# Two stacked gated layers behind an attention stage on one core: weight pieces loaded into their final buffers, the order of work found by a planner that repeats itself, and the first token block's steps split around the second's

## The chip, the cores and the metric

The kernel runs on one core of one Trainium2 chip. The metric is the device time of that core in microseconds. Engine names are those of the profile: PE is TensorE's matmul side (PEld its weight loads), DVE is VectorE, ACT is ScalarE, POOL is GpSimd, and SP is SyncE, which here only issues DMAs.

## What is computed

Four batches of eight heads (576 positions, 64 wide) go through two attentions whose outputs are added. One is a softmax attention on q, k, v averaged over groups of four positions, its output repeated four times. The other is a local softmax attention in which a position sees only neighbours less than four away. The sum is laid out as 2304 tokens by 512. Two feed-forward layers follow (512 to 2048 and back), the first with a sigmoid gate, the second with a rational function. Cut to what matters:

```
out_up = np.repeat(sm_attn(q_d, k_d, v_d), 4, axis=2)     # on means over 4 positions
scores = np.where(abs(i - j) < 4, scale * q @ k.T, -1e9)
x = (out_up + softmax(scores) @ v).transpose(0, 2, 1, 3).reshape(2304, 512)
h = x @ moe_w_in;  x = (h * sigmoid(h)) @ moe_w_out
h = x @ moe2_w_in; out = rational(h; a, b) @ moe2_w_out
```

The large weights arrive as 64-bit floats.

## The kernel before

**Stages.** The first stage is all of the attention and the first layer, woven together; the second stage is the second layer. A matmul in it keeps single precision by three products: every operand is split into a rounded high part and a low rest, and high times high, high times low and low times high are added in PSUM.

**Steps of the first stage.** The 2304 tokens are cut into five blocks, of 480 tokens four times and 384 once (`BLOCKS1`, in chunks of 96). A **step** is one block and one of the 16 slices `f` of 128 hidden columns; there are 80 of them (`STEP1`), block by block. Step s has an h part (`h_mm`, L739, 12 matmuls into `hps`), then on ACT a tanh (L890), on DVE the product with it (L893, `th<-th,hps`, which I use as the **mark** of the step because every step has exactly one), on ACT the high part `gh` and on DVE or POOL the low part `gl` (L902). Two steps later comes the o part (`o_mm`, L751, 12 matmuls that add into `acc`). After slice 15 the block's sums are copied out of PSUM (`o_out`) and stored (`o_store`) for the second stage.

**Pieces.** Each slice of each weight matrix is one piece: 32 of the first layer (`I` for w_in, `O` for w_out) and 32 of the second. `piece` loads the raw 64-bit words into a ring `raw` of three buffers and turns them into two single-precision parts: ACT takes the high words (L651) and the low words (L655), DVE clamps and shifts (L658, L660), DVE or POOL adds (L664), DVE merges (L667), ACT makes the rounded part (L286), DVE or POOL the rest (L675). A w_in piece stays on the chip in its home `w{f}`. A w_out piece goes to a ring `wo` of three, is used by its step in block 0 and is also stored to memory (`wos`), from where the later blocks reload it, once a step. Second-layer pieces go through a single buffer `cvo` to memory.

**Attention.** Six chunks of 96 tokens a batch. A chunk has scores on PE (L522, L531), a maximum on DVE (L537), exponentials on ACT (L547), sums on DVE (L552), a normalisation on DVE or POOL (L556), transposes on PE (L567), a copy, the product with v on PE (L582), the addition of the averaged attention's output on DVE (`ad`, L589, two instructions), then the high part `xh` on ACT and the low part `xl` (L603) on DVE or POOL. A batch also has the averaged attention (L423, L439, L444, L448, L457, L471) once. A block can begin when the chunks in its 480 tokens are through.

**What sets the order.** All of this is written as jobs with costs per engine, prerequisites, buffers and a due time. `Plan.run` walks through time and gives every free engine the ready job with the earliest due time; the instructions are then emitted in that order, and each engine runs its own in program order. Due times are constants here: step s is due at `HEAD` plus the sum of the steps before it, a block's attention `LEAD` = 45000 ns ahead of the block, a piece some 6000 ns ahead of its step in block 0. While the plan sees PE empty early on, filler matmuls (`warm`, L250) are put in.

## Time and profile before

| | |
|---|---|
| time, median of 3 runs | 934.55 us (934.46 to 936.43) |
| the profiled execution's own time | 939.73 us |
| its span, first to last instruction | 937.9 us |
| busy: PE, PEld, DVE, ACT, POOL | 909.9, 762.6, 706.6, 603.0, 333.6 us |
| busy tenths of DVE in 40 slices | 6899989863457667667332289998999899799995 |
| busy tenths of PE in 40 slices | 8997888999999999999999999999999999999997 |

The profiled execution took 5.2 us more than the median, and 1.8 us of its time lies outside the span. One slice of the 40 is 23.4 us. A 9 is 90% or more. The second stage begins at about 532 us, where the mark of step 79 is. PE's ends are modelled, so a stretch in which PE shows busy may still hold short waits.

### The profile page before, as it was taken

The numbers are of one execution on the slowest core, as the hardware profiler recorded it, in microseconds if no ns is written. First come the engines' busy times: TensorE is split into PE (matmuls) and PEld (weight loads), VectorE is DVE, ScalarE is ACT, GpSimd is POOL, SyncE is SP. The second block draws the span as 40 slices with busy tenths as digits, with TensorE's granted clock in tenths as the row PEclk, the third lists the DMA queues.
The fourth block names the chain that finished last, engine by engine and source line by source line (L and its number), as shares of the span: only waits on it lengthen the run. The fifth ranks groups of instructions, "written<-read, shape, count | busy, mean of one in ns | idle before, by whom it ended". The sixth has DMA issues, their size and how long they took to land.

```text
span 937.9 us, 16163 instructions
## 1 busy us (share of the span) xinstructions
PE 909.9 (97%) x6201; PEld 762.6 (81%) x6201; DVE 706.6 (75%) x1064; ACT 603.0 (64%) x1214; POOL 333.6 (36%) x279
## 2 busy tenths in 40 slices
PE   8997888999999999999999999999999999999997
PEld 6785666787888778887899988888888888899986
DVE  6899989863457667667332289998999899799995
ACT  4877757644345666555332378877877777788884
POOL 4532232212201132213000046655555546455553
PEclk9999988999999999999999999999999999999999
DMA  9886799688978668774966573002000200200000
GB/s 281 276 232 215 222 294 292 224 316 255 246 247 286 212 227 264 236 289 148 341 216 224 181 287 151 1 1 90 0 1 9 71 1 1 78 1 1 35 1 34
DMA packets 47497, 152.03 MB, mean 162 GB/s; under 512 B 5212, under 2 KB 9948, under 8 KB 47420
## 3 DMA queue, kind: packets, MB, share of 16 engines
q1 hardware_dynamic: 44972, 143.03, 43.8%
q0 software_dynamic: 2160, 7.96, 4.9%
q8 instruction: 49, 0.80, 0.4%
q14 instruction: 28, 0.23, 0.1%
q10 hardware_dynamic: 288, 0.00, 0.0%
HBM read 116.38 MB, written 34.60 MB: 161 GB/s over the span
## 4 chain that ended last, share of the span: by engine, by line
PE 83%; DVE 6%; DMA 5%; ACT 4%; issue 1%; POOL 0%; ACTq 0%; SPq 0%; DVEq 0%; POOLq 0%
PE hps L739 39%; PE acc L965 21%; PE acc L751 17%; DMA raw<-moe_w_in 3%; DMA raw<-moe_w_out 2%; DVE cw L667 1%; ACT E L547 1%; PE wps L250 1%; PE pair L531 1%; PE pair L582 1%; DVE cr L664 1%; ACT EE L439 1%; DVE cw L660 1%; DVE cw L658 1%; PE pair L567 1%
## 5 line engine op out<-in xcount | busy, mean ns | idle before, releaser
L751 PE MATMUL acc<-gh,wo 128*128 128x480 f32 (+1 forms) x640 | 204.8, 378 | 7.0 <-ACT wo L286 3.7
L739 PE MATMUL hps<-xh,w 128*128 128x480 f32 (+1 forms) x640 | 208.1, 384 | 1.0 <-ACT w L286 0.4
L739 PE MATMUL hps<-x2h,wi 128*128 128x512 f32 (+1 forms) x640 | 196.4, 368 | 0.0
L819 POOL TENSOR_TENSOR u<-u,ah 128x512 f32<-128x512 f32 (+1 forms) x80 | 96.1, 1201 | 261.7 <-ACT u L817 260.0
L965 PE MATMUL acc<-wo,gh 128*128 128x512 f32 x576 | 178.0, 390 | 0.0
L751 PEld LDWEIGHTS acc<-gh,wo 128*128 128x128 f32 x640 | 119.0, 188 | 27.5 <-ACT wo L286 5.7
L739 PEld LDWEIGHTS hps<-xh,w 128*128 128x128 f32 x640 | 121.1, 191 | 20.6 <-DVE w L675 1.3
L739 PEld LDWEIGHTS hps<-x2h,wi 128*128 128x128 f32 x640 | 118.9, 188 | 16.4
L996 POOL TENSOR_TENSOR gl<-p,gh 128x512 fp32r<-128x512 f32 (+1 forms) x80 | 120.9, 1511 | 11.6 <-issue 8.8
L965 PEld LDWEIGHTS acc<-wo,gh 128*128 128x128 f32 x576 | 107.7, 188 | 20.9
L739 PE MATMUL hps<-xl,w 128*128 128x480 f32 (+1 forms) x320 | 120.4, 376 | 0.0
L751 PE MATMUL acc<-gl,wo 128*128 128x480 f32 (+1 forms) x320 | 118.5, 370 | 0.0
L739 PE MATMUL hps<-x2l,wi 128*128 128x512 f32 (+1 forms) x320 | 117.7, 368 | 0.0
L965 PE MATMUL acc<-wo,gl 128*128 128x512 f32 x288 | 112.7, 391 | 0.0
L893 DVE SCALAR_TENSOR_TENSOR th<-th,hps 128x480 f32<-128x480 f32 (+1 forms) x80 | 50.4, 629 | 68.4 <-ACT th L890 67.8
L988 DVE SCALAR_TENSOR_TENSOR u<-u,r 128x512 f32<-128x512 f32 (+1 forms) x80 | 99.4, 1243 | 2.8
L890 ACT ACTIVATE th<-hps 128x480 f32<-128x480 f32 (+1 forms) x80 | 44.5, 557 | 87.5 <-PE hps L739 84.8
L981 ACT ACTIVATE r<-u,cst 128x512 f32<-128x512 f32 (+1 forms) x80 | 54.5, 682 | 52.7 <-POOL u L819 52.7
L987 DVE SCALAR_TENSOR_TENSOR u<-u,r 128x512 f32<-128x512 f32 (+1 forms) x80 | 83.5, 1043 | 0.5 <-ACT r L982 0.5
L664 POOL TENSOR_TENSOR cr<-cw,cr 128x512 int32<-128x512 int32 x25 | 33.8, 1353 | 137.4 <-DVE cw L660 96.6
L816 DVE TENSOR_TENSOR p<-p,hps 128x512 f32<-128x512 f32 (+1 forms) x80 | 50.5, 632 | 30.4 <-ACT p L815 30.3
L286 ACT ACTIVATE gh<-th 128x480 fp32r<-128x480 f32 (+1 forms) x79 | 46.6, 590 | 38.6 <-DVE th L893 27.4
(122 smaller groups left out, 1468.8 us busy)
## 6 DMA issues: line engine op xcount, KB each, us to landing
wo<-wos SPq DMA_DIRECT2D x64, 512.0 KB, 4.2
raw<-moe_w_in SPq DMA_DIRECT2D x32, 512.0 KB, 4.7
raw<-moe_w_out SPq DMA_DIRECT2D x32, 512.0 KB, 5.9
w2s<-cvo SPq DMA_DIRECT2D x32, 512.0 KB, 5.6
kq<-kq SPq DMA_DIRECT2D x12, 788.0 KB, 7.8
wos<-wo SPq DMA_DIRECT2D x16, 512.0 KB, 4.7
wi<-w2s SPq DMA_DIRECT2D x16, 512.0 KB, 7.8
wo<-w2s SPq DMA_DIRECT2D x16, 512.0 KB, 7.4
```

The costliest lines, as they stand in the source:

```text
L286: nc.scalar.activation(out, in_, AF.Copy, scale=scale)
L739: nc.tensor.matmul(hps[:, :n], lhsT=wi[:, i, 128 * g:128 * g + 128], rhs=(a, b)[s][:, g, :n], start=(m == 0), stop=(m == len(mms) - 1))
L751: nc.tensor.matmul(acc_t[j][g // 2][:, g % 2, :n], lhsT=wo[:, i, 128 * g:128 * g + 128], rhs=s_[:, :n], start=(f == 0 and m % 3 == 0), sto ...
L816: nc.vector.tensor_tensor(out=p, in0=p, in1=hps, op=ALU.mult)
L819: nc.gpsimd.tensor_tensor(out=u, in0=u, in1=ah, op=ALU.mult)
L890: nc.scalar.activation(x["t"][:, :n], x["h"][:, :n], AF.Tanh, scale=0.5)
L893: nc.vector.scalar_tensor_tensor(out=x["t"][:, :n], in0=x["t"][:, :n], scalar=1.0, in1=x["h"][:, :n], op0=ALU.add, op1=ALU.mult)
L965: nc.tensor.matmul(acc2[j][c], lhsT=a[:, 128 * c:128 * c + 128], rhs=wo[:, i, :], start=(f == 0 and m % 3 == 0), stop=(f == NF - 1 and m % ...
L981: nc.scalar.activation(r, u, AF.Ln, scale=2.0 ** -64, bias=cst[:, 0:1])
L987: nc.vector.scalar_tensor_tensor(out=u, in0=u, scalar=1.000001, in1=r, op0=ALU.add, op1=ALU.mult)
L988: nc.vector.scalar_tensor_tensor(out=u, in0=u, scalar=-2.0, in1=r, op0=ALU.add, op1=ALU.mult)
L996: nc.gpsimd.tensor_tensor(out=gl2[k_][:, :n], in0=p, in1=gh2[k_][:, :n], op=ALU.subtract)
```

## The change

- **Homes.** A raw piece is loaded straight into the buffer in which its result will lie: `w{f}` for a w_in piece, one of `NBUF` = 7 general buffers (`buf`) for any other. These 7 take the place of `raw` (3), `cvo` (1) and `wo` (3), at the same size in total; evicted block sums use them too. The conversion overwrites the raw words in place.
- **Plan.** Due times are now relative to the planned start of a step (`At`). Only the last job of a chain has one; `run` passes it back along the prerequisites, so that each job is due as late as its successors allow. `settle` plans six times, each time with the step starts that the last plan gave, and takes the plan whose PE work ends first. A reload of a `wo` piece is tied to the o part four steps before it (`AHEAD`).
- **Split.** Block 0 runs slices 0 to 7, then block 1 all 16, then block 0 slices 8 to 15, then blocks 2 to 4. Slices 8 to 15 are thus first used in block 1. Block 0's sums are copied out twice; the second time POOL issues DMAs that add to memory.
- **Addition on PE.** In batch 0 PE adds the averaged attention's output into the same PSUM tile by two matmuls with an identity (L634 of the new kernel) ahead of the product with v. `ad` is gone there, `xh` and `xl` are taken from PSUM, `xl` always on DVE.

```
+SPLIT = 8
+AHEAD = 4
...
-RING = 3
+NBUF = 7
...
-LEAD = 45000.0
+TAIL, STAG, STAG0 = 40000.0, 4000.0, 2000.0
+TAIL1 = 24000.0
+SAFE = 4000.0
+PRE = 3000.0
...
+UP_PE = 1
+ROUNDS = 6
...
+    def settle(self, when, rounds):
+        best, tried = None, []
+        for _ in range(rounds):
+            self.run(when)
+            tried.append((max(j.end for j in self.jobs if j.eng == "P"), len(tried), when))
+            when = [j.start for j in self.jobs if j.step is not None]
+        return self.run(min(tried)[2])
...
+        for j in reversed(self.jobs):
+            for d in j.after:
+                d.t = min(d.t, j.t - self.LAT - min(d.cost.values()) -
+                          (d.size / self.DMA_RATE + self.DMA_LAT + PRE if d.size else 0.0))
...
-            pool.sort(key=lambda j: j.due)
+            pool.sort(key=lambda j: j.t)
...
+    PART1 = [(0, 0, SPLIT), (1, 0, NF), (0, SPLIT, NF)] + [(j, 0, NF) for j in range(2, len(BLOCKS1))]
+    STEP1 = [(j, f) for j, lo, hi in PART1 for f in range(lo, hi)]
+    part1 = [p for p, (j, lo, hi) in enumerate(PART1) for f in range(lo, hi)]
+    first1 = [STEP1.index((0 if f < SPLIT else 1, f)) for f in range(NF)]
...
-        due0 = when[first * NF] - LEAD
+        d0 = FAR
...
-            d0 = when[j * NF] - LEAD + 250.0 * i
+            due = begin[j] - (TAIL1 if j == 1 else TAIL) - (STAG if j else STAG0) * (BLOCKS1[j] - 1 - i)
...
+                if b < UP_PE:
+                    for a in range(2):
+                        nc.tensor.matmul(op[:, a, :2 * CH], lhsT=ident,
+                                         rhs=upt[0].rearrange("p (m a) q -> p a m q", a=2)[:, a, :, 24 * c:24 * c + 24]
+                                         .unsqueeze(3).to_broadcast([128, 2, 24, 4]), start=True, stop=False)
...
-                                                 start=True, stop=True)
+                                                 start=b >= UP_PE, stop=b >= UP_PE or m + s_ == 2)
...
+                if b < UP_PE:
+                    x["x"] = x["o"][:, :, :2 * CH].rearrange("p a (m q) -> p a m q", m=2)
+                    sl = slice(CH * i, CH * i + CH)
+                    x["h"], x["l"] = (t[j].rearrange("p (m a) q -> p a m q", a=2)[:, :, :, sl] for t in (xh, xl))
+                else:
+                    x["h"], x["l"] = (t[j][:, :, CH * i:CH * i + CH] for t in (xh, xl))
+                copy(e, x["h"], x["x"])
+            def lo(e, x=x):
+                eng(e).tensor_tensor(out=x["l"], in0=x["x"], in1=x["h"], op=ALU.subtract)
...
+            ja = jo if pe else plan.add(f"A{b}{c}", d0, {"V": 2 * v_ns(192)}, ad, after=[jo], give=[pO, upu])
+            jh = plan.add(f"H{b}{c}", d0, {"A": a_ns(384), "V": v_ns(384)} if pe else {"A": a_ns(384, False), "V": 300}, hi, port=not pe, after=[ja] + x_first.get(j, []),
...
-    for name, n in (("raw", 3), ("cw", 3), ("cr", 2), ("cvo", 1), ("wo", RING)):
+    for name, n in (("buf", NBUF), ("cw", 3), ("cr", 2)):
...
+    def buf(u, name, shape=(128, 2, DM), dtype=F32R):
+        return cv.tile(list(shape), dtype, tag=f"buf{u.no}", name=name, bufs=1)
...
-            x["raw"] = cv.tile([128, DM, 2], I32, tag="raw", name="raw", bufs=3)
+            if home.ring == "buf":
+                x["raw"] = buf(home, "raw", (128, DM, 2), I32)
+            else:
+                x["raw"] = wp.tile([128, DM, 2], I32, tag=home.ring, name="raw")
...
-        j0 = plan.add(f"{name}.l", due - 12000, {"D": 60}, ld, take=[ru] + ([dst_unit] if dst_unit in wo_u.values() else []),
-                      size=128 * 4096)
...
+        j0 = plan.add(f"{name}.l", FAR, {"D": 60}, ld, take=[home], size=128 * 4096)
...
+        j7 = plan.add(f"{name}.7", due - SAFE, {"V": 610, "G": 1270}, c7, after=[j6], give=[wu], port=True)
...
+        p = part1[s]
+        f0, f1 = PART1[p][1:]
...
+                             start=(f == f0 and m % 3 == 0), stop=(f == f1 - 1 and m % 3 == 2))
...
+    def o_store(p, i):
+        j, f0, _ = PART1[p]
         n = BLOCKS1[j] * CH
-        if g % 2 == 0:
-            xe_t[j, g // 2] = cv.tile([128, 2, DM], F32, tag="raw", name="xe", bufs=3)
-        copy(e, xe_t[j, g // 2][:, g % 2, :n], acc_t[j][g // 2][:, g % 2, :n], 0.5)
-    def o_store(j, i):
-        n = BLOCKS1[j] * CH
-        nc.sync.dma_start(out=x2s[2 * i:2 * i + 2, :, tok0[j]:tok0[j] + n].rearrange("g p n -> p g n"),
-                          in_=xe_t[j, i][:, :, :n])
+        o = x2s[2 * i:2 * i + 2, :, tok0[j]:tok0[j] + n].rearrange("g p n -> p g n")
+        if f0:
+            nc.gpsimd.dma_start(out=o, in_=xe_t[p, i][:, :, :n], accum_op=ALU.add)
+        else:
+            nc.sync.dma_start(out=o, in_=xe_t[p, i][:, :, :n])
...
+                        stores[j, g // 2] = plan.add(f"x{p}.s{g}", due, {"G": 1000} if f0 else {"D": 60},
+                                                     lambda e, p=p, i=g // 2: o_store(p, i),
+                                                     after=cps[-1:] + ([stores[j, g // 2]] if f0 else []), give=[xu],
+                                                     size=128 * 4096, early=1e9)
...
-                                       after=[wos_job[f], wo_job[NF - 1]], take=[wo_u[s]], size=128 * 4096)
+                                       after=[wos_job[f]], take=[wo_u[s]], size=128 * 4096)
...
+        for s in range(AHEAD, ns):
+            f = STEP1[s][1]
+            j = load_wo[f] if s == first1[f] else wos_load[s]
+            if s - AHEAD in done_o:
+                j.after.append(done_o[s - AHEAD])
...
-    order = plan.run()
+    order = plan.settle(guess, ROUNDS)
```

Three places show how instructions moved. The first is DVE from the mark of step 10 on. In the kernel before (`cw`, `cr`, `raw`, `w`, `wo` are pieces, `xs`, `n`, `r`, `E` attention):

```order
L893 SCALAR_TENSOR_TENSOR th<-th,hps 128x480
L658 TENSOR_SCALAR cw<-cw 128x512
L660 TENSOR_SCALAR cw<-cw 128x512
L675 TENSOR_TENSOR w_1907<-cw,w_1907 128x512
L902 TENSOR_TENSOR gl<-th,gh 128x480
L664 ISA cr<-cw,cr 128x1024
L537 TENSOR_REDUCE n_1936<-pair 128x8
L667 SCALAR_TENSOR_TENSOR cw<-raw,cr 128x512
L282 CAST wo<-cw 128x512
L675 TENSOR_TENSOR wo<-cw,wo 128x512
L552 TENSOR_REDUCE r_1980<-E_101 128x8
L553 RECIPROCAL r_1980<-r_1980 128x8
```

And the same place in the changed kernel, where step 10 is block 1's slice 2 (L986 is the mark, L995 `gl`, L739 to L756 pieces):

```order
L986 SCALAR_TENSOR_TENSOR th<-th,hps 128x480
L995 TENSOR_TENSOR gl<-th,gh 128x480
L756 TENSOR_TENSOR w_1881<-cw,w_1881 128x512
L748 SCALAR_TENSOR_TENSOR cw<-raw,cr 128x512
L739 TENSOR_SCALAR cw<-cw 128x512
L741 TENSOR_SCALAR cw<-cw 128x512
L986 SCALAR_TENSOR_TENSOR th<-th,hps 128x480
L756 TENSOR_TENSOR w_1919<-cw,w_1919 128x512
L745 ISA cr<-cw,cr 128x1024
L995 TENSOR_TENSOR gl<-th,gh 128x480
```

Before, these rows do not yet reach the mark of step 11; after, they pass it.

The second place is SP around the first reloads of w_out pieces (`wo<-wos`). Before:

```order
L643 DMA raw<-moe_w_out 128x1024
L714 DMA wos<-wo 128x1024
L643 DMA raw<-moe_w_in 128x1024
L643 DMA raw<-moe_w_out 128x1024
L723 DMA w2s<-cvo 128x1024
L865 DMA wo<-wos 128x1024
L714 DMA wos<-wo 128x1024
L865 DMA wo<-wos 128x1024
```

After:

```order
L724 DMA raw<-moe_w_in 128x1024 x2
L795 DMA wos<-wo 128x1024
L568 DMA vw<-vw 128x512 x2
L958 DMA wo<-wos 128x1024
L724 DMA raw<-moe_w_in 128x1024
L795 DMA wos<-wo 128x1024
L958 DMA wo<-wos 128x1024
L443 DMA vd<-vp 72x1024
L958 DMA wo<-wos 128x1024
```

The first reload moved from the 84th DMA on SP to the 49th, with 20 of the first layer's 32 raw pieces issued ahead of it instead of all 32.

The third place is PE at batch 0's first product with v, before the first step. Before, with filler around it:

```order
L250 LDWEIGHTS wz
L250 MATMUL wps<-wz 128x256
L582 MATMUL pair<-PT,vw_288 64x48 x16
L582 MATMUL acc<-PT,vw_288 64x48 x16
L250 LDWEIGHTS wz
```

After:

```order
L634 MATMUL pair<-up,ident 128x192 x2
L643 MATMUL pair<-PT,vw_288 64x48 x16
L634 MATMUL acc<-up,ident 128x192 x2
L643 MATMUL acc<-PT,vw_288 64x48 x16
L634 MATMUL pair<-up,ident 128x192 x2
```

Two identity matmuls now precede each product, and the first five chunks' products stand in one run.

## Rows read from the trace of the kernel before

**Rows 1.** Busy time by stretch: us, each engine's busy (instructions), PEclk, DMA share, GB/s.

```profile
50.30:107.00 56.70, 48.53 (x346) 36.08 (x344) 53.31 (x96) 39.87 (x91) 16.92 (x16) 1.00 0.69 215
107.00:179.00 72.00, 63.49 (x621) 48.42 (x620) 62.85 (x114) 48.98 (x114) 24.86 (x21) 0.91 0.87 267
179.00:224.90 45.90, 45.90 (x295) 37.73 (x294) 24.21 (x44) 21.75 (x41) 3.51 (x3) 1.00 0.88 290
224.90:317.30 92.40, 92.40 (x619) 76.88 (x617) 55.39 (x99) 46.34 (x100) 16.60 (x15) 1.00 0.80 255
317.30:468.00 150.70, 149.19 (x1287) 121.41 (x1284) 95.65 (x179) 83.23 (x201) 33.35 (x27) 1.00 0.72 247
468.00:532.20 64.20, 64.20 (x363) 63.58 (x362) 19.11 (x34) 17.34 (x35) 0.00 (x0) 1.00 0.66 228
...
0.00:201.00 201.00, 179.27 (x1893) 138.99 (x1894) 173.31 (x323) 136.37 (x345) 67.69 (x76) 0.97 0.82 258
```

**Rows 2.** First of these stretches, L893 (the marks) alone: DVE busy (count).

```profile
50.30:107.00 56.70, 5.17 (x8) 1.00 0.69 215
```

**Rows 3.** Waits of PE, 50.3 to 179 us: who, for whom, us, times, longest.

```profile
PE acc L751 <- ACT wo L286: 3.7, 5, 1.3
PE pair L567 <- DVE xs L589: 3.4, 2, 2.6
PE acc L751 <- DVE wo L675: 1.8, 4, 0.8
```

**Rows 4.** DVE's groups by line and shape: xcount | busy us, mean ns | idle before.

```profile
L667 DVE SCALAR_TENSOR_TENSOR cw<-raw,cr 128x512 int32<-128x512 int32 x64 | 47.3, 740 | 2.5 <-POOL cr L664 2.2
L893 DVE SCALAR_TENSOR_TENSOR th<-th,hps 128x480 f32<-128x480 f32 x64 | 41.5, 648 | 29.3 <-ACT th L890 28.7
L902 DVE TENSOR_TENSOR gl<-th,gh 128x480 fp32r<-128x480 f32 x54 | 37.8, 700 | 23.4 <-ACT gh L286 23.1
...
L660 DVE TENSOR_SCALAR cw<-cw 128x512 int32<-128x512 int32 x64 | 28.9, 452 | 2.2
...
L664 DVE CUSTOM_DVE_ANT_0 cr<-cw,cr 128x1024 uint16<-128x1024 uint16 x39 | 27.4, 704 | 0.5
...
L552 DVE TENSOR_REDUCE r<-E 128x8 f32<-128x440 f32 x24 | 14.6, 607 | 8.0 <-ACT E L547 7.9
...
L589 DVE TENSOR_TENSOR xs<-pair,up 128x192 f32<-128x192 f32 x42 | 13.0, 351 | 11.6 <-PE pair L582 11.4
...
L603 DVE TENSOR_TENSOR xl<-xs,xh 128x384 fp32r<-128x384 f32 x20 | 12.1, 606 | 2.6 <-ACT xh L286 2.4
...
L675 DVE TENSOR_TENSOR wo<-cw,wo 128x512 fp32r<-128x512 f32 x12 | 8.5, 712 | 0.1
...
L444 DVE TENSOR_REDUCE r<-EE 128x6 f32<-128x870 f32 x8 | 8.4, 1048 | 0.8 <-ACT EE L439 0.8
```

**Rows 5.** Timeline of PE: attention's groups of matmuls (start us, us).

```profile
30.55 1.20 PE L471 MATMUL pair<-PT,vd 72*64 72x144 f32 x16 [0.21 <-ACT PT L286]
...
41.35 0.69 PE L531 MATMUL pair<-kq 64*64 64x54 f32 x32
...
42.95 0.68 PE L582 MATMUL acc<-PT,vw 54*64 54x48 f32 x32
...
78.19 0.97 PE L423 MATMUL pair<-kqd 64*64 64x144 f32 x24
...
100.20 0.45 PE L457 MATMUL pair<-ident,EE 48*72 48x48 f32 x12 [0.29 <-ACT EE L439]
```

**Rows 6.** Chain of work that ended last: start us, us, what.

```profile
260.16 2.60 PE acc L751 x12
```

**Rows 7.** Timeline of PE where the granted clock fell.

```profile
136.34 0.66 PE L567 MATMUL pair<-ident,E 48*128 48x48 f32 x8 [2.60 <-DVE xs L589]
...
140.48 1.17 PE L739 MATMUL hps<-xh,w 128*128 128x480 f32 x2
```

**Rows 8.** Busy time by stretch there, columns as in rows 1.

```profile
130.00:140.00 10.00, 6.74 (x100) 4.86 (x91) 6.89 (x16) 5.12 (x11) 4.54 (x4) 0.77 0.93 297
```

More of the change, by code (lines that the diff above doesn't have):

```diff
@@ L84, in __init__, with run @@
     def __init__(self):
-        self.jobs, self.rings, self.lent = [], {}, {}
+        self.jobs, self.sizes, self.lends = [], {}, {}
     def ring(self, name, n):
-        self.rings[name] = list(range(n))
+        self.sizes[name] = n
     def add(self, *a, **k):
         j = Job(*a, **k)
-        for u in j.give:
-            u.left += 1
         self.jobs.append(j)
         return j
-    def run(self):
+    def settle(self, when, rounds):
[5 more added lines that the diff above has]
+        return self.run(min(tried)[2])
+    def run(self, when):
         users = {}
+        self.rings = {k: list(range(n)) for k, n in self.sizes.items()}
+        self.lent = dict(self.lends)
         for j in self.jobs:
+            for u in j.give:
+                u.left = 0
+        for j in self.jobs:
+            j.start = j.end = j.eng = None
+            j.t = when[j.due.step] + j.due.ns
+            for u in j.give:
+                u.left += 1
+        for j in reversed(self.jobs):
+            for d in j.after:
+                d.t = min(d.t, j.t - self.LAT - min(d.cost.values()) -
+                          (d.size / self.DMA_RATE + self.DMA_LAT + PRE if d.size else 0.0))
             j.wait = len(j.after)
@@ L347, in ld @@
                 nc.sync.dma_start(out=kqt[t], in_=kq[b, t])
-            loads.append(plan.add(f"L{b}{t}", due0 - (9000 if b == 0 else 0) + 100 * t, {"D": 60}, ld, take=[u],
+            loads.append(plan.add(f"L{b}{t}", FAR, {"D": 60}, ld, take=[u],
                                   size=128 * 4 * 1576))
@@ L363, in sm @@
                         nc.vector.tensor_reduce(out=o, in_=i.rearrange("p g (j r) -> p g j r", r=4), axis=AX.X, op=ALU.add)
-                    sums.append(plan.add(f"R{b}{t}{w}", due0 - 6000, {"V": v_ns(768)}, sm, after=[loads[t]] + sums[:1],
+                    sums.append(plan.add(f"R{b}{t}{w}", FAR, {"V": v_ns(768)}, sm, after=[loads[t]] + sums[:1],
                                          take=[] if sums else [kdu], give=[kqu[t]]))
@@ L624, in attention @@
             x_done.setdefault(j, []).append(
-                plan.add(f"X{b}{c}", d0, {"V": v_ns(384), "G": g_ns(384)}, lo, after=[jh], give=[xu], port=True))
+                plan.add(f"X{b}{c}", due, {"V": v_ns(384)} if pe else {"V": v_ns(384), "G": g_ns(384)}, lo, after=[jh],
+                         give=[pO] if pe else [xu], port=not pe))
+    takes = {}
     xh, xl, x_u, x_first, x_done = {}, {}, {}, {}, {}
@@ L670, in c6 @@
         def c6(e):
-            x["hl"] = dst()
+            x["hl"] = dst(home)
             copy(e, x["hl"][:, 0], x["w"])
@@ L744, in o_mm @@
         n = BLOCKS1[j] * CH
-        if f == 0 and lo == 0:
-            acc_t[j] = [ps.tile([128, 2, 512], F32, tag="acc", name="acc", bufs=2) for _ in range(2)]
+        p = part1[s]
+        f0, f1 = PART1[p][1:]
+        if f == f0 and lo == 0:
+            acc_t[p] = [ps.tile([128, 2, 512], F32, tag="acc", name="acc", bufs=2) for _ in range(2)]
         wo, gh, gl = wo_t[s], gh_t[s], gl_t[s]
@@ L832, in o_jobs @@
             n = BLOCKS1[j] * CH
-            due = when[s] + 2.2 * (when[1] - when[0])
-            if f == 0:
-                accs[j] = [Unit("acc"), Unit("acc")]
+            due = when[s] + 12000
+            p = part1[s]
+            f0, f1 = PART1[p][1:]
+            if f == f0:
+                accs[p] = [Unit("acc"), Unit("acc")]
             for i in range(4):
@@ L912, in moe1 @@
                 prev_h = plan.add(f"h{s}.{i}", when[s] + i, {"P": r_ns(n, 3)}, hm, after=after, take=[hu] if i == 0 else [],
-                                  give=[x_u[j]] if f == NF - 1 and i == 3 else [], closes=s == 0)
+                                  give=[x_u[j]] if f == NF - 1 and i == 3 else [], closes=s == 0, step=s if i == 0 else None)
             jt = plan.add(f"th{s}", when[s], {"A": a_ns(n)}, th, after=[prev_h], take=[tu])
```

157 lines of the change are left out of this document (89 added, 68 removed).

## The prediction

> **What bounds the kernel now.** I read the page's slices first: DVE stands at 8 or 9 from the second to the eighth slice while PE dips in the fourth to the seventh, and after that PE is full. So I cut the first stage at the marks (one L893 per step) of steps 0, 8, 16, 24, 40, 64 and 79 and asked for busy time in each stretch [rows 1]. The marks alone show that the first stretch holds eight steps [rows 2]. Its 56.7 us have DVE busy 53.31 and PE 48.53; the next eight steps take 72.0 us with DVE busy 62.85. From 179 us on PE is busy all the time but for 1.51 us in the stretch 317.3 to 468.0. What PE waits for in steps 0 to 15 is mostly weight pieces (`wo`) from ACT and DVE, and once for 2.6 us the addition `xs` [rows 3]. So DVE sets the pace of block 0, where all 32 first-layer pieces must be converted within 16 steps, and PE sets it after that.
>
> **PE's own need.** Twelve matmuls of 480 columns take 2.60 us [rows 6], so a step costs 5.2 us, and a step of 384 columns 4.2. Attention's groups come on top [rows 5]: scores 0.69, product with v 0.68, averaged scores 0.97, its product with v 1.20, a group of transposes 0.45; for a chunk's band matmuls I take 0.36, my estimate from half of a score group. I counted the matmuls between marks in both kernels' order. In the three stretches from 179.0 to 468.0, where PE was the bound, these durations give 249.5 us of steps and 35.0 of attention; busy was 45.9 + 92.4 + 149.2 = 287.5, that is 38.0 for attention, so I raise attention by 9%. Before, steps 0 to 8 need 39.1 us of h and o parts and 6 of attention, 45 in all, and steps 8 to 16 need 39.1 + 16 = 55. Against 56.7 and 72.0 that is 11.6 and 17 us lost, and 1.5 later: **30 us in all**. More than these 30 the change cannot take from the first stage, and it does not touch the second.
>
> **Split, part by part.** What moves is when DVE must have done what. The changed order, priced by rows 4, has between marks 0 and 8: 28 clamps and shifts (12.7 us), 10 adds L664 (7.0), 13 merges (9.6), 7 rests (5.0), 8 marks (5.2), 7 `gl` (4.9), 8 `ad` (2.8), 5 `xl` (3.0), 8 maxima and sums of attention with their reciprocals (7.4, a maximum taken like the sum), 3 normalisations (2.7, taken like the sums of the same sizes): 60.3 us. The same count before gives 58.2 for this stretch and 65.3 for the next; busy was 53.31 and 62.85, because neighbours overlap, so such a sum is worth 0.94 of itself. The changed kernel then needs of DVE 56.7 us for steps 0 to 8, and (sums 27.3, 43.7, 73.9, 103.7) 26, 41, 70 and 98 for steps 8 to 16, 16 to 24, 24 to 40 and 40 to 64. ACT, by the same counting, sums to 55.9 in the first stretch against 47.5 before, worth 47.
>
> So the crowd does not leave steps 0 to 8: attention for block 1 has moved into them (ten chunks' outputs are through by mark 8, six before) while the number of merged pieces is 18 against 17. It leaves steps 8 to 16, which hold 6 merges and no attention.
>
> PE's need in the changed order, counted the same way: steps 0 to 8: 39.7 + 15.1 = 54.8; 8 to 16: 38.4; 16 to 24: 41.7 + 6.0 = 47.7; 24 to 40: 83.3 + 20.9 = 104.2; 40 to 64: 124.5 + 19.6 = 144.1; 64 to 79: 63.2. That is 452.4, as before (451.7): nothing is saved on PE.
>
> **The waits that stay.** In steps 0 to 8 DVE (56.7) and PE (54.8) are nearly equal. Before, the stretch took 3.4 us more than DVE's busy time when PE had slack, and the next one 9.2 more. I take 6, between the two and nearer the first, where the clock held: 62.7, with bounds of 57 and 66. In steps 8 to 16 there is one new thing, the turn from block 0 to block 1: the accumulators must be copied out before block 1's o part begins. Its bounds are 0, as at the later turns, where PE showed full [rows 1], and 2.6, the longest wait of PE [rows 3]; I take 1.5: 39.9. Steps 16 to 24 then have DVE at 41 of 47.7 and ACT as full: I add 1.0. Steps 24 to 40 hold more attention than before and the second eviction: 1.2 more. Steps 40 to 64 keep the 1.5 of before. Sum: 62.7 + 39.9 + 48.7 + 105.4 + 145.6 + 63.2 = 465.5 against 481.9: **16.4 us less**.
>
> **Edits that I cost at little.** Loading into homes removes no instruction; it frees loads from the ring of three, and what it is worth is in the stretches above. The split adds two copies on ACT and two on DVE and two adding DMAs on POOL, behind which a `gl` and a piece are queued; POOL is busy 16.60 of 92.40 us where they fall [rows 1], and the second stage reads their result some 200 us later. The identity matmuls: no row shows one. Nearest are 8 matmuls of 144 columns in 1.20 us (0.20 for 192 columns) and 12 in 0.97 (0.11); upward, four passes at the 480-column rate would be 0.35. For two of them 0.2 to 0.7 us. Five of the six chunks stand before step 0, where PE runs filler; the sixth costs at most 0.7 inside steps 0 to 8. They spare DVE the two `ad` of 0.35 a chunk, but `xl` is now always DVE's (0.61) [rows 4]. Before mark 0 the DVE sum falls from 44.8 to 42.7 and ACT's from 46.0 to 45.7, so the first step may begin up to 2 us earlier, or as much later if the product with v now waits on PE's run of identities: I take 1 earlier.
>
> Together 17.4 us. The profiled execution, 939.73, would be 922.3; that run lies 5.2 above the median, so against the median 934.55 I forecast **917** (own range 911 to 924).
>
> **Rivals.**
>
> *The first eight steps stay crowded.* Three engines close to full, each in program order, could lose as steps 8 to 16 did before: 72.0 for 55 of PE, that is 17. Then steps 0 to 8 take 72 and the gain is 8: 927. For it speaks that ACT's sum grew by 8; against it that the clock's fall is part of those 17.
> *Memory.* By the reload of step 24 the changed kernel must have moved 48 MB on SP's queue and some 7 MB of adding DMAs on POOL's (sizes and places from the order), 55 MB; by my stretches that reload is due near 201 us, 274 GB/s. Before, 258 GB/s was reached to that point with the DMA engines 82% busy, and 290 at 88% at best over a long stretch [rows 1]; at full share that is 315 to 330. If no more than the 258 of before is reached, step 24 comes 12 us late: 929. The Trainium skill (DMA: Bandwidth & Descriptors, Specifications) puts the memory limit of a core at about 358 GB/s; by that, an estimate, 55 MB take 154 us and nothing would wait. No stretch of rows 1 comes above 290, so the row is the stricter one.
>
> *It closes up better.* With 57 in the first stretch and no new waits, the sum is 455 and the time 906.
>
> *Slower: the clock.* After PE waited 2.6 us, two of its matmuls spanned 1.17 us [rows 7], where 2.60 for twelve makes 0.43 and a tail, and the granted clock averaged 0.77 over 10 us [rows 8]: the lower of its two levels, 1.2 GHz, for part of it. If waits of that length come in each of steps 2 to 8, half of the stretch's 54.8 us of PE work at the lower level costs 27 us and eats the gain: 945. It decides from about 17 us of PE work at the lower level. Against it: in 50.3 to 107 PE waited often, but shortly, and the granted clock was 1.00 [rows 1]. The Trainium skill (TensorE: Matmul & The Clock Gate, What's actually happening) has the lower clock as the default and activity as what releases it; by that rule a fuller PE, as forecast here, keeps 2.4 GHz, and rows 1 agree with it.
>
> **How the numbers follow.** Forecast 0.53; better 0.13; crowded 0.14; memory 0.11; slower 0.09. Of the crowded and memory cases about a fifth would end within 0.2% (1.9 us, about what a measurement of this kernel can tell from no change). So faster 0.86, same 0.05, slower 0.09. The range reaches to the better case's 905 and past the crowded and memory cases to 930.
>
> **What would show it.** In the changed profile, the stretch between marks 0 and 8 should take 60 to 66 us with DVE busy near 57, that from 8 to 16 about 40 with PE full and DVE near 26, and mark 24 should come near 201 us instead of 224.9. Waits of PE for `wo` and `w` after 115 us should be gone. I am wrong if mark 8 comes after 118 us (crowded), if PE waits for `wo` from a DMA between 115 and 200 us (memory), if the granted clock dips before mark 24, or if new waits turn up past step 24, where I have allowed under 3 us.

## The result and the profile after

The changed kernel takes 925.63 us (median of 4 runs, 923.69 to 929.13), the kernel before, measured beside it, 935.11 (4 runs, 934.46 to 936.43): a ratio of 0.9898, 95% interval 0.9880 to 0.9916, or 9.5 us less. The forecast was 917 with a range of 905 to 930. The profiled execution of the changed kernel took 925.38 us, its span is 923.6 us (before 937.9).

The marks (start of the product with the tanh, now L986, in us from the start of the span):

| mark of step | 0 | 8 | 16 | 24 | 40 | 64 | 79 | from there to the end |
|---|---|---|---|---|---|---|---|---|
| before | 50.3 | 107.1 | 179.0 | 224.9 | 317.3 | 468.0 | 532.2 | 405.6 |
| after | 51.5 | 114.3 | 152.3 | 202.0 | 309.4 | 453.4 | 516.6 | 407.1 |

The stretches between these marks, in the form of [rows 1]: start and end, length, busy time (instructions) of PE, PEld, DVE, ACT and POOL, the granted clock, the DMA engines' share, GB/s.

```profile
51.50:114.30 62.80, 58.69 (x580) 44.96 (x579) 56.36 (x102) 46.97 (x105) 21.38 (x19) 0.97 0.78 252
114.30:152.30 38.00, 38.00 (x176) 32.82 (x175) 25.35 (x45) 19.42 (x35) 6.76 (x7) 1.00 0.98 314
152.30:202.00 49.70, 48.45 (x356) 39.43 (x354) 43.62 (x73) 37.31 (x92) 21.65 (x15) 1.00 0.70 244
202.00:309.40 107.40, 105.59 (x960) 84.55 (x959) 72.83 (x127) 61.55 (x153) 31.53 (x27) 1.00 0.85 263
309.40:453.40 144.00, 144.00 (x1134) 118.31 (x1134) 97.75 (x175) 79.67 (x173) 20.33 (x16) 1.00 0.80 278
453.40:516.60 63.20, 63.20 (x357) 62.59 (x356) 17.95 (x33) 16.28 (x33) 0.00 (x0) 1.00 0.55 191
```

The stretch of steps 8 to 16, which took 72.0 us, takes 38.0 with PE never idle; those of steps 0 to 8, 16 to 24 and 24 to 40 have become longer, the first by 6.1 us, and the last two shorter, by 6.7 and 1.0. What PE waits for in steps 0 to 24, in the form of [rows 3]:

```profile
PE pair L472 <- ACT EE L488: 1.7, 1, 1.7
PE acc L834 <- DVE gl L995: 1.4, 1, 1.4
PE pair L520 <- ACT PT L333: 0.7, 1, 0.7
...
PE hps L820 <- DVE th L986: 1.2, 1, 1.2
```

No wait for `wo` is left. After mark 24 come two more (1.2 us with no releaser, 0.6 for `PT`), after mark 40 none. The second stage did not change: from its first h matmul (518.93 us, before 533.55) to the end it takes 404.67 us (404.35), with PE busy 399.55 in both. Of the 1.5 us more in the last column of the table, 1.1 are o parts that now stand behind mark 79 (518.93 is 2.4 us behind it, 533.55 was 1.3), about as much as steps 64 to 79 take less.

### The profile page after: what moved, and what is told of

It is laid out like the page before. It is cut to its first block, busy times and chain, and to the rows that moved or that the text cites. A ratio compares the mean times of both kernels' runs of the same rounds, so it can differ in the third digit from the quotient of the medians.

```text
span 923.6 us, 16147 instructions
## 1 busy us (share of the span) xinstructions
PE 906.0 (98%) x6189; PEld 762.9 (83%) x6189; DVE 708.9 (77%) x1047; ACT 605.7 (66%) x1222; POOL 339.7 (37%) x282
## 4 chain that ended last, share of the span: by engine, by line
PE 90%; DVE 5%; ACT 3%; issue 1%; DMA 1%; POOL 0%; SPq 0%; ACTq 0%; DVEq 0%; POOLq 0%
PE hps L820 42%; PE acc L1067 21%; PE acc L834 20%; PE pair L643 1%; PE wps L290 1%; PE pair L582 1%; PE pair L520 1%; DVE cw L748 1%; ACT E L598 1%; PE pair L618 1%; ACT EE L488 1%; DMA raw<-moe_w_in 1%; DVE gl L995 0%; PE pair L506 0%; DVE cw L741 0%
## 5 line engine op out<-in xcount | busy, mean ns | idle before, releaser
L820 PE MATMUL hps<-xh,w 128*128 128x480 f32 (+1 forms) x640 | 224.4, 380 | 1.2 <-DVE th L986 1.2
L834 PE MATMUL acc<-gh,wo 128*128 128x480 f32 (+1 forms) x640 | 223.8, 378 | 0.0
L834 PEld LDWEIGHTS acc<-gh,wo 128*128 128x128 f32 x640 | 120.3, 188 | 17.4 <-issue 1.6
L983 ACT ACTIVATE th<-hps 128x480 f32<-128x480 f32 (+1 forms) x80 | 44.6, 557 | 108.3 <-PE hps L820 105.4
L986 DVE SCALAR_TENSOR_TENSOR th<-th,hps 128x480 f32<-128x480 f32 (+1 forms) x80 | 50.3, 629 | 82.0 <-ACT th L983 81.5
L745 POOL TENSOR_TENSOR cr<-cw,cr 128x512 int32<-128x512 int32 x27 | 36.7, 1361 | 119.2 <-ACT cr L736 38.8
L820 PEld LDWEIGHTS hps<-x2l,wi 128*128 128x128 f32 x320 | 60.1, 188 | 8.8
```

The costliest lines, as they stand in the source:

```text
L745: eng(e).tensor_tensor(out=x["r"], in0=x["w"].bitcast(I32), in1=x["r"], op=ALU.add)
L820: nc.tensor.matmul(hps[:, :n], lhsT=wi[:, i, 128 * g:128 * g + 128], rhs=(a, b)[s][:, g, :n], start=(m == 0), stop=(m == len(mms) - 1))
L834: nc.tensor.matmul(acc_t[p][g // 2][:, g % 2, :n], lhsT=wo[:, i, 128 * g:128 * g + 128], rhs=s_[:, :n], start=(f == f0 and m % 3 == 0), st ...
L983: nc.scalar.activation(x["t"][:, :n], x["h"][:, :n], AF.Tanh, scale=0.5)
L986: nc.vector.scalar_tensor_tensor(out=x["t"][:, :n], in0=x["t"][:, :n], scalar=1.0, in1=x["h"][:, :n], op0=ALU.add, op1=ALU.mult)
```

## A ledger of PE's lost time

The experiments become readable with three numbers a kernel, taken up to mark 79. **Idle** is the length of a stretch less PE's busy time in it. **Clock** is the time lost to the lower granted clock: one less the granted clock, times the length, added over pieces of about 5 us. What is left of mark 79 after both is what the profile shows as PE's work, fillers included. Each row is one profiled execution; the last column is the median of the kernel's runs.

| kernel (us) | idle: head, 0-8, 8-16, 16-79 | clock: head, 0-8, 8-16, 16-79 | mark 79 | less both | time, median |
|---|---|---|---|---|---|
| before | 5.1, 8.2, 8.5, 1.5 | 0, 0, 6.8, 0 | 532.2 | 502.1 | 935.11 |
| before, again | 4.7, 6.5, 9.6, 0.4 | 1.7, 0, 6.8, 0 | 530.6 | 500.9 | 936.00 |
| **after** | 5.3, 4.1, 0, 3.0 | 1.7, 1.7, 0, 0 | 516.6 | 500.8 | 925.63 |
| copies | 5.1, 4.1, 0, 3.0 | 1.7, 1.7, 0, 0 | 516.2 | 500.6 | 925.25 |
| no identity | 7.9, 4.1, 0, 0 | 0, 1.7, 0, 0 | 514.3 | 500.6 | 925.05 |
| no split (16) | 5.2, 2.9, 8.9, 0 | 1.7, 0, 3.4, 0 | 525.1 | 503.0 | 933.68 |
| split at 6 | 6.5, 8.9, 0, 1.4 | 1.7, 6.9, 0, 0 | 524.7 | 499.3 | 934.21 |
| split at 10 | 6.1, 6.7, 4.3, 0.9 | 0, 5.1, 3.4, 0 | 527.3 | 500.8 | 937.05 |
| clamp twice | 4.6, 5.8, 0.3, 6.1 | 0, 5.1, 0, 3.4 | 525.1 | 499.8 | 934.50 |
| no clamp | 6.0, 3.5, 0, 2.6 | 1.7, 0, 0, 0 | 513.3 | 499.5 | 923.44 |
| ACT twice | 4.4, 7.2, 0, 5.1 | 5.1, 3.3, 0, 1.7 | 527.7 | 500.9 | 936.92 |
| fill one wait | 5.0, 3.4, 0, 3.0 | 1.7, 0, 0, 0 | 514.9 | 501.8 | 923.69 |
| fill two waits | 5.8, 3.4, 0, 3.0 | 0, 0, 0, 0 | 515.8 | 503.6 | 925.64 |
| fill, no identity | 7.9, 2.4, 0, 0 | 0, 3.4, 0, 0 | 516.1 | 502.4 | 923.25 |

The work is 499 to 504 us in every one of them, while mark 79 moves by 18.9 us. So most of what a variant gained or lost up to mark 79 is idle time and clock, and the clock's share comes in portions of about 1.7 us. Differences of a few us in the last but one column are not explained by this. Of the 15.6 us by which mark 79 came earlier, 10.9 are idle time, 3.4 are clock, and 1.3 are the difference in the last but one column.

## The experiments

**The kernel before once more**, for the spread of its executions.

> The kernel before once more, unchanged. Theory (its profiled execution was a bad sample): its span of 937.9 us went with a granted clock of 0.993, and the other executions lie 4 to 5 us lower; then the spans and clocks listed for the new runs fall on a line, a lower clock with a longer span, the median stays near 935 us, and a new profile shows steps 8 to 16 shorter than 71.9 us, because part of those was the clock's fall at 133 to 150 us. Rival (profiling itself costs 5 us): the new profile is again near 938 us with the same fall.

936.00 us (12 runs, 933.78 to 939.88), ratio 0.9997 (0.9982 to 1.0011); the profiled span is 936.2, and steps 8 to 16 take 72.2 us again, with 6.8 of clock in them. So the theory fell where it called that stretch a bad sample: both profiled executions have its falls. It also fell in the line of clock and span: at a granted clock of 0.995 alone, the spans of these 12 runs go from 931.9 to 938.0 us. Not every execution loses as much: a clock of 0.996, which some have, leaves some 4 us for all falls together, where the ledger has 6.8 and 8.5. The rival, a cost of profiling, is not borne out either: the profiled executions of the changed kernel, of the kernel without identity matmuls and of that without the clamp lie below their medians. What stands is that the execution that the sum was made against, 939.73, was near the top of what this kernel does: all its other runs lie between 932.33 and 940.71, and the medians of their groups between 934.6 and 936.3.

**Memory: extra copies.**

```
 nc.sync.dma_start(out=new_wo(s), in_=wos[f])              # L958, reload of step s
+if s < 24: nc.sync.dma_start(out=xtra[s], in_=wos[f])     # 8 of them, memory to memory
```

> Behind each of the 8 reloads of a weight tile for steps 8 to 15 (line 958) SP issues a copy of the same 512 KB in memory that nobody reads: 4 copies in the stretch of steps 0 to 8 and 4 in that of steps 8 to 16, each read and written. Theory (the DMA engines have room though they show a share of 0.98 in steps 8 to 16, where PE is never idle): marks 8, 16 and 24 move by less than 2 us each and the time by less than 2. Rival (314 GB/s in that stretch is all there is): 2 MB read and 2 MB written at 314 GB/s are 6 to 13 us; marks 16 and 24 come 6 to 13 us later, with PE waiting for weight tiles from a DMA.

925.25 us (4 runs, 923.29 to 925.57), 0.9875 (0.9859 to 0.9890). The stretch of steps 8 to 16 in this kernel:

```profile
114.00:151.90 37.90, 37.90 (x176) 32.75 (x175) 24.96 (x44) 19.23 (x35) 7.57 (x8) 1.00 1.03 357
```

It moved 357 GB/s where the changed kernel moved 314, and PE was still never idle. A reload landed 13.3 us after its issue (median) instead of 9.0, and nothing waited for it. The DMA share of 0.98 was no limit; the memory rival falls, and by a margin. The Trainium skill (DMA: Bandwidth & Descriptors, Specifications) gives about 358 GB/s as a core's limit. This run came up to that over 37.9 us, and the changed kernel goes above it in its head, so over 10 us it does not hold here:

```profile
20.00:25.00 5.00, 3.91 (x68) 2.82 (x67) 4.93 (x8) 4.93 (x21) 4.63 (x7) 1.00 1.00 380
25.00:30.00 5.00, 4.16 (x96) 3.03 (x92) 4.17 (x10) 4.91 (x17) 3.28 (x2) 1.00 1.01 407
```

**The identity matmuls.** `UP_PE = 0`: the averaged output is added on DVE in the first batch too.

> The changed kernel with the addition in batch 0 back on DVE (UP_PE 0); homes, plan and split stay. Theory: the identities take 0.65 to 0.85 us a chunk on PE, five of them in one run on the way to step 0, and spare DVE about 0.7 a chunk, so the two cancel: within 3 us of the changed kernel's 925.6, and mark 0 within 2 us of 51.5. Rival (the identities delay the start): mark 0 comes 3 us earlier or more and the time falls to 922 or less. Other rival (they carry part of the gain): 929 or more.

925.05 us (4 runs, 923.16 to 926.94), 0.9873 (0.9850 to 0.9896): no difference from the changed kernel that these runs can tell. Their price does show, in the chain of work of the changed kernel (start us, us, what):

```profile
36.68 0.85 PE acc L634 x4
...
52.18 0.65 PE pair L634 x4
```

0.65 to 0.85 us a chunk, five of the six on the chain that leads to the first step. In the ledger PE is idle 2.6 us longer in the head without them, but loses 1.7 less to the clock there, and 3.0 us of idle time after mark 16 are gone. That they spare the wait for `ad`, and that the two cancel, fits this but was not tested by itself.

**No split.** `SPLIT = 16`: block 0 whole, then block 1; homes and new plan as they are.

> The changed kernel with block 0 run in one piece (SPLIT 16); homes, plan and identities stay, the plan is made anew for it. Theory (the split carries the gain, because it takes half of the pieces out of block 0): steps 0 to 16 take at least 118 us instead of 101 and the time is 932 to 938. Rival (the plan and the homes carry it): 924 to 928, with steps 0 to 16 below 106 us.

933.68 us (9 runs, 931.07 to 936.07), 0.9965 (0.9949 to 0.9981). Its first two stretches:

```profile
51.40:97.40 46.00, 43.10 (x249) 34.34 (x248) 45.27 (x84) 32.23 (x63) 10.39 (x10) 1.00 0.91 281
97.40:172.80 75.40, 66.45 (x685) 50.80 (x685) 64.81 (x116) 52.69 (x136) 24.80 (x21) 0.95 0.80 256
```

121.4 us for steps 0 to 16, where the changed kernel takes 100.8 and the one before 128.7. Some of the difference is attention that then lies later (steps 16 to 24 take 42.2 us here, 49.7 with the split), but 6 to 8 of the 9.5 us hang on the split (6 by the two ratios, 8 by the medians); homes, plan and identity matmuls together are worth 2 to 5 us without it. The theory was right about both numbers. No run has the split without the homes or without the repeated plan, so what each of these adds to it is not shown.

**Other places for the split.** `SPLIT = 6` and `SPLIT = 10`.

> The first block is split after 6 steps instead of 8. Steps 0 to 5 and 12 to 21 then bring new weight pieces. Theory (what counts is how many pieces and how much of attention DVE must finish in the first stretch): DVE's 56.4 us fall by 4 pieces and two steps' marks and `gl`, some 12 us, PE's by 10, so the ratio of the two stays near that of now and the ten steps with new pieces later have DVE near 51 of 58 us: 923 to 928, no clear difference from the split at 8. Rival (an earlier block 1 is short of attention's output): PE waits for `xh`, `xl` before step 6, 928 to 934.

> The first block is split after 10 steps instead of 8. With the split at 6 PE was idle 8.9 us in the first eight steps and the clock's falls took 6.9 there. Theory (what an earlier block 1 brings forward is attention for it; a later one gives ACT and DVE two more steps of PE's time for the same groups, but two more steps of pieces): idle time of PE in steps 0 to 10 stays near the 4.1 us of now, time 923 to 928. Rival (the split at 8 is a lucky order, and any other loses some 8 us, as at 6 and at 16): 931 to 936.

934.21 us (7 runs, 932.46 to 934.67), 0.9972 (0.9961 to 0.9982) at 6, and 937.05 us (10 runs, 935.18 to 938.21), 1.0003 (0.9986 to 1.0021) at 10. My theory fell both times: it counted how much the engines have to do in a stretch, and by that count all three splits are alike. The stretches of steps 0 to 8 at 6, and of steps 0 to 8 and 8 to 16 at 10:

```profile
53.30:120.90 67.60, 58.65 (x488) 44.87 (x489) 59.17 (x102) 45.25 (x95) 17.84 (x15) 0.90 0.80 254
```

```profile
48.80:118.70 69.90, 63.25 (x619) 48.80 (x620) 59.79 (x105) 47.42 (x118) 25.18 (x20) 0.93 0.75 240
118.70:167.10 48.40, 44.07 (x277) 36.62 (x276) 33.04 (x62) 25.68 (x58) 7.53 (x7) 0.93 0.82 273
```

What PE waited for in the first stretches, at 6 and then at 10:

```profile
PE hps L820 <- DVE th L986: 3.0, 1, 3.0
PE hps L820 <- ACT xh L333: 2.0, 1, 2.0
PE hps L820 <- DVE w L756: 1.6, 1, 1.6
```

```profile
PE pair L643 <- ACT E L598: 4.1, 2, 2.9
PE pair L573 <- ACT EE L488: 3.5, 1, 3.5
PE hps L820 <- DVE th L986: 3.0, 1, 3.0
```

Single waits of 1.6 to 3.5 us, nearly each for something else, with the clock falling behind most of them. At 6 the rival's wait is among them: the 2.0 us for `xh`, at 107 us, hold the first h part of block 1, and 0.4 for `xl` follow, of 8.9 us idle. Idle and clock together take 15.8 us of steps 0 to 16 at 6 and 19.5 at 10, against 5.8 at 8. So a split is not worth this by itself; this split in the order that the planner happens to find for it is. Why that order meets fewer late producers than its neighbours was not settled.

**DVE from both sides.** The clamp of a piece (L739, DVE) issued twice, and left out.

```
 nc.vector.tensor_scalar(out=x["w"], in0=x["w"], scalar1=W_LOW, scalar2=W_HIGH, op0=ALU.max, op1=ALU.min)
+nc.vector.tensor_scalar(the same)       # clamp twice; in the other kernel the first line is gone
```

> The changed kernel with the clamp of each piece (0.44 us on DVE) done twice, order of all else kept; the second clamp changes nothing in the result. Steps 0 to 8 hold 14 of the 64, 6.2 us. Theory (DVE sets the pace of steps 0 to 8): that stretch grows by 5 to 6.5 us, steps 8 to 16 by under 1, the rest together by under 4; time 931 to 936. Rival (PE or waits between engines set it): under 3 us there, time under 929.

> The clamp of a piece (line 739, the first of two DVE instructions of that step) is left out; weights below 2^-15 are then not rounded as the reference has them. It is the mirror of the doubled clamp: 14 times 0.418 = 5.9 us less of DVE in steps 0 to 8. Theory (DVE is late there, PE next): the stretch of 62.8 us falls by 3 to 5, to 58 to 60, where PE's own 54.8 to 58.7 us stop it; steps 16 to 40, where the doubled clamp cost 6, give back at most the 1.2 and 1.8 us in which PE is idle. Whole time 918 to 922. Rival (the engines are balanced and the doubled clamp only made a new bound): nothing changes, 924 to 926.

Twice: 934.50 us (10 runs, 931.85 to 936.74), 0.9981 (0.9965 to 0.9998). Without: 923.44 us (4 runs, 922.20 to 925.28), 0.9861 (0.9844 to 0.9878). The first stretch, twice and without:

```profile
50.10:117.00 66.90, 61.06 (x576) 46.77 (x577) 63.31 (x116) 46.29 (x104) 21.89 (x19) 0.92 0.78 247
```

```profile
51.20:111.10 59.90, 56.39 (x575) 43.25 (x574) 51.55 (x89) 46.64 (x106) 21.09 (x19) 1.00 0.83 259
```

With 7 us more of DVE the stretch grows by 4.1, which is 1.7 more of idle time, 3.4 more of the clock and 1.0 less of the rest; with 4.8 us less it shrinks by 2.9, of which 1.7 are one fall of the clock less and 0.6 idle time. More work on DVE does delay PE; less work gives back little, because PE itself has 56 to 57 us of work there. The time rose by 8.9 us; mark 79 came 8.5 later, with 4.4 more of idle time, 5.1 more of the clock and 1.0 less of the rest. In steps 40 to 79 the doubled clamp costs nothing (207.4 us, after 207.1), but steps 16 to 40 take 6.1 us more, where the theory had under 4 for all the rest. Steps 16 to 24 of that kernel:

```profile
154.60:208.40 53.80, 50.05 (x358) 40.51 (x360) 48.85 (x85) 37.55 (x92) 21.25 (x15) 0.97 0.63 228
```

So the forecast time of 931 to 936 came, but with less than forecast in the first stretch. Without the clamp the stretch came as the theory had it (58 to 60), and the time lies between the theory's 918 to 922 and the rival's 924 to 926.

**ACT.** Its conversion of a piece's low words (L736) issued twice.

```
 nc.scalar.activation(x["r"], x["raw"][:, :, 0].bitcast(U32), AF.Copy, scale=2.0 ** -29)
+nc.scalar.activation(the same)
```

> ACT's conversion of a piece's low half (line 736, `cr` from `raw`) is issued twice; DVE's and PE's work is unchanged. Theory (DVE sets the pace of steps 0 to 8 and ACT has room: busy 46.97 of 62.80 us there): about 14 more conversions fall into steps 0 to 8, some 8 us of ACT, of which at most 2 us show in that stretch, and 0 to 4 us in the whole time. Rival (ACT paces these steps as much as DVE, because it stands in every piece's chain): the stretch grows by 5 to 8 us and the time by 7 to 10, as with the doubled clamp on DVE (+4.1 and +8.9).

936.92 us (10 runs, 935.08 to 937.58), 1.0002 (0.9990 to 1.0014): the whole gain is gone. The first stretch, and that of steps 16 to 24:

```profile
55.30:121.20 65.90, 58.70 (x557) 44.38 (x550) 57.16 (x102) 54.86 (x119) 21.59 (x19) 0.95 0.80 249
159.70:212.70 53.00, 50.02 (x354) 40.72 (x352) 43.80 (x73) 45.18 (x104) 20.82 (x15) 0.97 0.64 231
```

The stretch grew by 3.1 us, short of the rival's 5 to 8, but the head grew by 3.8 and steps 16 to 24 by 3.3, and the whole by 11.3. So the theory that ACT has room falls, though it was busy for only 46.97 of 62.80 us. Here the idle time of an engine that runs in program order was not a reserve, since its results are waited for one by one. Of mark 79's 11.1 us, 4.3 are idle time and 6.7 clock.

**Fillers against the falls.** In the changed kernel, 2 us at a time (columns as above):

```profile
80.00:82.00 2.00, 1.81 (x29) 1.12 (x27) 1.97 (x4) 2.00 (x4) 1.83 (x2) 1.00 0.11 45
82.00:84.00 2.00, 1.26 (x21) 0.98 (x17) 2.00 (x3) 1.39 (x4) 0.40 (x1) 1.00 0.40 158
84.00:86.00 2.00, 1.91 (x15) 1.01 (x15) 1.97 (x5) 1.52 (x4) 0.00 (x0) 0.64 1.02 307
86.00:88.00 2.00, 2.00 (x14) 1.64 (x9) 1.97 (x5) 1.13 (x2) 0.00 (x0) 0.51 0.95 364
88.00:90.00 2.00, 2.00 (x20) 1.48 (x19) 1.85 (x4) 0.97 (x2) 0.00 (x0) 1.00 1.03 414
```

PE is partly idle up to 84 us; the clock falls to 0.5, that is to 1.2 GHz, after PE is busy again, and the work that was waited for then runs at half speed. The edit puts matmuls of no use ahead of waits that were seen in the trace; one kernel fills a wait in step 5, the next also one in the head.

```
+FILL = {"S11": (13, None), "t101": (2, 5), "o10": (6, 5)}   # job: fillers, step whose hps takes them
 ...
+if x.name in FILL: warm(n, into the accumulator that this step's h part will overwrite)
 x.emit(x.eng)
```

> 8 filler matmuls (128 x 256 in bf16, 0.11 us each) are put into PE's program in step 5, 2 before a group of transposes and 6 before the product with the averaged v that waited 0.74 us for ACT at 82.08 us; they write an accumulator that the next h part overwrites. Nothing else changes. In the changed kernel PE was busy 3.07 of the 4 us from 80 to 84, and from 84.4 to about 88 the granted clock was near 0.5, which cost 1.7 us. Theory (the clock falls after a stretch in which PE was partly idle, and the fall costs as much again as the wait): no fall near 85 us, the stretch of steps 0 to 8 is 1 to 2 us shorter, time 923.5 to 925. Rival (the fall has nothing to do with this wait): the fall stays, and the fillers that do not fit the wait add 0 to 0.4 us.

923.69 us (6 runs, 923.24 to 925.15), 0.9866 (0.9840 to 0.9891). The stretch of steps 0 to 8, the same 4 us and those after:

```profile
51.00:112.60 61.60, 58.16 (x586) 44.48 (x586) 55.92 (x101) 46.99 (x105) 21.99 (x19) 1.00 0.80 258
...
80.00:82.00 2.00, 2.00 (x28) 1.36 (x23) 1.97 (x4) 2.00 (x5) 1.73 (x2) 1.00 0.04 14
82.00:84.00 2.00, 1.94 (x21) 1.18 (x18) 2.00 (x4) 1.39 (x3) 0.00 (x0) 1.00 0.68 240
84.00:86.00 2.00, 1.72 (x17) 1.19 (x18) 1.93 (x5) 1.51 (x4) 0.00 (x0) 1.00 0.99 277
86.00:88.00 2.00, 2.00 (x20) 1.47 (x19) 2.00 (x5) 1.26 (x3) 0.00 (x0) 1.00 1.01 372
```

The fall is gone, and the stretch of steps 0 to 8 takes 61.6 us instead of 62.8. The time is 1.9 us lower by the medians, but the intervals of the two ratios overlap. The place is what tells: a fall stands there, between 84 and 90 us, in all three profiles of the split at 8 without fillers and with the clamp and ACT's work as they were (the changed kernel, copies, no identity), and in none of the three with fillers.

> As the run with 8 fillers in step 5, and 13 more before the second band scores of block 1, which waited 1.5 us at 44.34 us ahead of the other fall (47 to 50.5 us). Theory: both falls go, the first stage ends 2.5 to 3.5 us earlier, time 921.5 to 923.5. Rival (that wait, for which the profile names no releaser, is not one that fillers can hide): the fillers run after or before it and add up to 1.4 us, time 924.5 to 926.5.

925.64 us (6 runs, 924.58 to 928.93), 0.9887 (0.9861 to 0.9913). In the profile both falls are gone, but the wait in the head was not filled. The waits of PE there, 40 to 54 us, in the changed kernel and with the 13 fillers (with the 8 fillers alone, the first of these waits is 1.2):

```profile
PE acc L582 <- issue: 1.5, 1, 1.5
```

```profile
PE wps L293 <- issue: 1.3, 1, 1.3
```

Five of the 13 fillers run, then PE stands still for 1.3 us ahead of the sixth, with no releaser named, and the fillers come on top of the wait. Whatever holds PE there holds a filler as well as the scores; what it is stays open. That the fall behind this wait is gone need not be the fillers' doing: the head of the kernel before shows a fall in one of its two profiles. The rival was right about this one.

> The kernel without the identity matmuls (both outputs of attention added on DVE in the first batch too), with 14 filler matmuls (0.11 us each, 1.5 us) ahead of the product with the averaged v that waited 1.68 us for ACT at 82.96 us there; its granted clock then fell to 0.50 at 86 to 88 us (1.7 us lost). A second place and a longer wait for the test of the fillers, and the version meant to be the fastest. Theory (the clock falls after PE's idle time, and fillers hold it): no fall near 86 us, the stretch of steps 0 to 8 is 1.5 to 2.5 us shorter than 62.1, time 922 to 924 against 925.05 without fillers. Rival (the earlier run lost its fall by chance): the fall is there again, time 925 or more.

The edit is `UP_PE = 0` with `FILL = {"o10": (14, 5)}`.

923.25 us (4 runs, 921.72 to 924.91), 0.9848 (0.9820 to 0.9876). No fall near 86 us, as at the first place; the same 2 us in the kernel without fillers, then in this one:

```profile
86.00:88.00 2.00, 2.00 (x6) 1.50 (x5) 1.97 (x5) 0.53 (x2) 0.00 (x0) 0.50 1.08 235
```

```profile
86.00:88.00 2.00, 1.94 (x26) 1.46 (x22) 1.25 (x3) 2.00 (x5) 1.70 (x2) 1.00 0.11 37
```

The stretch of steps 0 to 8 did not become shorter than 62.1 us, as forecast, but took 63.4. The profiled execution lost 3.4 us to the clock elsewhere, behind a wait of 3.0 us that the kernel without fillers also has, there with no fall behind it (50 to 55 and 55 to 60 us in this kernel, then 50 to 55 in that without fillers):

```profile
50.00:55.00 5.00, 1.98 (x7) 1.37 (x6) 4.79 (x9) 4.23 (x13) 2.68 (x4) 0.78 0.81 279
55.00:60.00 5.00, 5.00 (x24) 3.66 (x23) 0.69 (x2) 1.27 (x3) 1.77 (x2) 0.54 1.00 249
```

```profile
50.00:55.00 5.00, 2.03 (x9) 1.80 (x10) 4.26 (x9) 3.75 (x12) 2.75 (x4) 1.00 0.76 269
```

The same wait, and in one execution the clock falls behind it and in another not. Two of the four runs had a granted clock of 0.999 over the span, and these took 921.72 and 921.96 us. By its median this is the fastest kernel of the study, 12.8 us under the one before; of its lead over the changed kernel (their intervals just miss each other, each against its own runs of the kernel before) leaving out the identity matmuls carries nothing that can be seen, and the fillers 1.8 to 1.9 us by the medians.

## Why the prediction was right, and where it was off

**The first stage was right, in sum and in its parts.** The six stretches were forecast at 62.7, 39.9, 48.7, 105.4, 145.6 and 63.2 us and took 62.8, 38.0, 49.7, 107.4, 144.0 and 63.2: 465.1 against 465.5. The signs named beforehand came: DVE 56.36 busy in the first stretch (forecast near 57) and 25.35 in the second (26), PE full there, no waits for `wo` or `w`, mark 24 at 202.0 (201), waits behind it of 1.8 us (under 3). Of the signs against me one came, the clock's dip before mark 24.

**Two sizes inside it were wrong and cancelled.** PE's own work between marks 0 and 79, busy time less clock, is 58.69 - 1.7 + 38.00 + 48.45 + 105.59 + 144.00 + 63.20 = 456.2, not 452.4; 2.2 of that is in the first stretch (57.0 for 54.8), where the short matmuls of attention lie between the long ones. The kernel before has the same excess: 456.9 by this reckoning where I had 451.7, so what it lost behind mark 0 was 25.0 us and not the 30 that I took as the most that could be gained. In the difference of the two kernels this error drops out. The waits that I allowed, 13.1 in all, came to 8.9, the clock among them; that they were too high by about what PE's work was too low is luck. In the first stretch I had DVE's 56.7 and 6 on top; what the ledger shows is PE 57.0, idle 4.1, clock 1.7. Same number, other reason: the runs without the clamp and with ACT doubled show three engines near balance, not DVE ahead. The rows held a hint: by them PE waited "mostly" for weight pieces in steps 0 to 15, but of 16.1 us that the profile lists there 7.7 were for pieces, and 8.4 for attention, much of that on ACT:

```profile
PE pair L457 <- ACT EE L439: 1.6, 2, 1.3
PE pair L423 <- ACT EE L439: 1.5, 1, 1.5
```

**The turn between blocks** was taken at 1.5 us and cost nothing: PE has no idle time in steps 8 to 16. **The head** was forecast 1 us earlier; its first h matmul stood at 46.45 us in both kernels, and the first mark 1.2 later, because the clock fell between the two:

```profile
45.00:50.00 5.00, 4.16 (x39) 3.55 (x40) 4.58 (x9) 3.55 (x16) 0.05 (x1) 0.70 1.06 327
```

**What missed was the step from the sum to the time.** The sum said 17.4 us. The span of the profiled executions fell by 14.3: 16.8 between the marks, less 1.2 of the head and 1.5 behind mark 79, to which I had given nothing (0.2 is rounding). The median fell by only 9.5 to 10.4, by which of the medians of before one takes. I had written that the profiled run "lies 5.2 above the median" and then took the whole sum off the median. The sum was made of that run's waits and falls, and such terms differ from one execution to the next: 23.3 us idle and 6.8 clock in the run that I read, and whole times from 932.33 to 940.71. Applied to the run that it was read from, the sum gives 939.73 - 17.4 = 922.3, which is 3 us from the 925.38 of the profiled execution. So the 8.6 us between the forecast of 917 and the measured 925.63 are 5.2 of the base, 3.1 of the sum (the head 2.2 later than forecast and 1.4 at the end, less 0.5 that the stretches did better), and 0.3 between that execution and its median. How the waits divide in an execution of the kernel before near its median no profile shows: both that were taken lie above it.

**The rivals.** The measured time is nearest to the 927 of the crowded first steps, but not by its mechanism: that one had the stretch at 72, and it took 62.8. The memory rival was shown wrong by the copies. "Closes up better" had no new waits and 57 in the first stretch; neither came. The slower case, the clock, is right as a mechanism: the clock did fall twice before mark 24, which I had named as a sign against me. It cost 3.4 us instead of 27 and took less than in the kernel before (6.8). Its point of decision, 17 us, was reached in no run; with ACT doubled the falls cost 10.1 us, and with 4.3 more of idle time nothing was left of the gain.

## What to carry to other kernels

Split the time of a PE-bound stretch into PE's work, its idle time and what the clock took; here the first moved by under 5 us in 14 profiles, so most of an edit's effect could be read by the other two, and 0.9 us of idle time cost 2.6 where the clock fell behind it. Where a wait can't be removed, a few useless matmuls ahead of the waiting instruction may cost nothing and hold the clock, but only if the filler itself is free to run. Before an engine that is 75% busy is called a reserve, double one of its instructions and look: here ACT's reserve was not there, and the best order lay between two neighbours that gave nearly all of the gain back, which no count of work had told.
